# Key-value sums with v stationary in both 64-column halves of the PE array, turned back by ten PE transposes

## The chip, the cores and the metric

One core of a Trainium2 chip. The metric is the device time of one execution in microseconds (us), taken as the median of several. The profile of an execution has a span that is about 1.7 us shorter than its time.

Engines are called PE (TensorE matmul), PEld (its weight load), DVE (VectorE), ACT (ScalarE), POOL (GpSimd) and SP (SyncE, which issues the DMAs). PSUM is the memory to which PE writes its results; the kernel uses it as eight banks.

## The reference, cut to what matters

S is 2048 tokens, D is 640, 32 heads of 20 columns each. Only the key-value sums are changed:

```python
xn = layernorm(x)
q, k, v = split(xn @ wqkv)                       # 32 heads of 20
pk = einsum("hsd,hdf->hsf", k, w_phi)
phi_k = concat([softmax(pk), softmax(-pk)])      # per head 2 x 20 features: e+ and e-
kv = einsum("hsf,hsd->hfd", phi_k, v)            # the key-value sums
z  = einsum("hsf->hf", phi_k)
o  = (phi_q @ kv) / (phi_q @ z + 1e-6)
out = x + o @ wo + (silu(xn @ w1) * (xn @ w3)) @ w2
```

## The kernel before

All operations go through a small list scheduler in the kernel. Several streams (norms, attention, MLP tiles, output tiles and so on) each offer their next step; the scheduler estimates when each could start and commits the earliest. So an MLP tile (ten weight loads and ten matmuls, about 2.16 us of PE) is what fills PE whenever the attention stream is not ready. It also means that a change of one stage can move MLP tiles elsewhere.

The tokens are on the partitions. `ekt` holds the normalized e+ and e- of all tokens, `v2` holds v with a column of ones after each head's 20 columns (21 per head), so that the sum with the ones gives z. The kernel before makes e stationary and moves v, a full block of 128 features against the 7 or 8 heads that touch it, and masks out (`GM`) the products of features with foreign heads on the way to `KVc`, which the query tiles read:

```python
def kv_sum(sg, fc, k):                      # sg: e+ or e-; fc: one of five 128-feature chunks
    h0, h1 = heads_of_chunk(fc)
    nh = h1 - h0 + 1
    for t in range(T):                      # 16 tiles of 128 tokens
        mm(bank(k, 21 * nh), ekt[:, t, sg, fc * 128:(fc + 1) * 128],
           v2[:, t, 21 * h0:21 * (h1 + 1)], t == 0, t == T - 1)
    pv = bank(k, 21 * nh).rearrange("p (h c) -> p h c", c=21)
    g = GM[:, fc, h0:h1 + 1]
    kv = KVc[:, sg, fc, 0:22 * nh].rearrange("p (h c) -> p h c", c=22)
    tt("DVE", kv[:, :, 0:DH], pv[:, :, 0:DH], g.unsqueeze(2).to_broadcast([128, nh, DH]), ALU.mult)
    stt(kv[:, :, DH], pv[:, :, DH], DEN_EPS if sg == 0 else 0.0, g, ALU.add, ALU.mult)
    copy("POOL", kv[:, :, DH + 1], g)
```

The late constants and the attention stream around the sums:

```python
def consts_late():
    memset("POOL", v2[:].rearrange("p t (h c) -> p t h c", c=21)[:, :, :, DH], 1.0)
# ... attention():
    while done["n"] < T:                    # all keys normalized (POOL)
        yield None
    for fc in range(DC):
        for sg in range(2):
            yield lambda fc=fc, sg=sg: kv_sum(sg, fc, banks(1))
    done["kv"] = 1
    # ... loads of w2 and of two x tiles, then per token tile: q_tok (12 matmuls against KVc), q_proj
```

A warm-up keeps PE busy while the first tiles of x arrive. In this kernel it happens to contain, beside full 128x512 matmuls, pairs with 63 columns stationary in either half of the array and 120 columns moving: the very form that the change brings into use.

```python
for _ in range(8):
    for q in range(2):
        mm(PS[64 * q:64 * q + 63, 3584:3584 + 120], z[:, 0:63], z[:, 120 * q:120 * q + 120], True, True)
```

The softmax here doesn't subtract the row's maximum and nothing guards it: scores larger than these inputs give would overflow.

## Time and profile before

The time before was 281.79 us (median of 3, 281.46 to 282.14).

| stage of the profiled run | us from the start | what PE does |
|---|---|---|
| x loads, LN, first projections | 0 to 40 | waits for x in places |
| k and v projections, query projection | 40 to 73 | no gaps |
| four MLP tiles | 73 to 82 | fill, while the attention stream waits for POOL, which normalizes the keys |
| key-value sums | 82.15 to 92.82 | 160 matmuls |
| query tiles, projections, MLP tiles | 93 to 213 | no gaps |
| output tiles alone | 213 to 281 | no gaps |

The page of the kernel before: the span, the busy time of each engine, and the chain of waits (what ended last, followed back), by engine.

```profile
span 280.8 us, 4674 instructions
...
PE 274.1 (98%) x1905; PEld 169.5 (60%) x1923; DVE 182.5 (65%) x321; ACT 105.5 (38%) x190; POOL 59.2 (21%) x90
...
PE 95%; DMA 2%; SPq 1%; DVE 1%; issue 1%; ACT 0%
```

PE is busy 98% of the span and makes up 95% of the chain. A busy PE need not be a limit, because records of pipelined matmuls overlap (that of a 512-column matmul is 379 ns long, and the next starts after 216); that the chain runs through PE with breaks of only 0.05 us from 40.5 us on is the stronger sign.

The timeline of PE in the kernel before (start us, length us, what, count; neighbours of one kind are merged under the first one's shape):

```profile
6.28 1.06 PE L101 MATMUL PS<-t 128*63 128x120 bf16 x19
...
77.84 4.48 PE L101 MATMUL PS<-xnT,w_s 128*128 128x512 bf16 x19
82.15 10.83 PE L101 MATMUL PS<-v,ekt 128*128 128x147 bf16 x160
93.03 2.11 PE L101 MATMUL PS<-xnT,w_s 128*128 128x512 bf16 x9
94.98 0.85 PE L101 MATMUL PS<-KVc,EqT 128*128 128x154 bf16 x12
```

The whole stage is the second of the lower four lines. `PS<-xnT,w_s` are MLP tiles, `PS<-KVc,EqT` is the first query tile. One MLP tile between the sums and the first query tile is enough to wait for KVc. `x9` is a tile of ten of which the trace lacks one record, and it is the first one: from the start of the last sum to the first MLP record there are 281 ns, one sum of 64 and one 512-column matmul of 216 more. A later run has the kernel before with a change elsewhere (`e4_before_late_selects`); its trace has all ten records and confirms it, 82.78 to 93.44 us:

```profile
82.78 10.83 PE L101 MATMUL PS<-v,ekt 128*128 128x147 bf16 x160
93.44 2.32 PE L101 MATMUL PS<-xnT,w_s 128*128 128x512 bf16 x10
```

The other engines around the same stage, and POOL earlier on:

```profile
51.43 2.37 POOL L101 MEMSET v<- 128x512 bf16 x1
...
53.90 0.71 ACT L101 ACTIVATE v<-PS 128x640 bf16<-128x640 f32 x1 [0.48 <-POOL v L101]
...
54.40 27.05 POOL L101 TENSOR_TENSOR ekt<-ekt,rS 128x640 bf16<-128x640 bf16 x22 [0.60 <-DVE rS L101]
...
93.02 0.30 DVE L101 TENSOR_TENSOR KVc<-PS,GM 128x140 bf16<-128x140 f32 x1 [0.51 <-PE PS L101]
...
93.61 0.22 POOL L101 COPY KVc<-GM 128x7 bf16<-128x7 bf16 x1 [0.82 <-DVE KVc L101]
```

The square brackets give the idle time before an instruction and what ended it. KVc is complete at 93.83 us, 0.8 us after the last matmul. POOL's normalization of the keys (54.40 + 27.05) ends at 81.45 us, just before the sums can begin. The memset of the ones in `v2` sits in the middle of it, and ACT's copy of v waited 0.48 us for that.

### The profile page before, as it was taken

How to read it: one execution, taken by the hardware profiler on the slowest of the kernel's cores; microseconds unless marked ns; L12 is line 12 of the kernel's file. 1: busy time of each engine (PE TensorE's matmuls, PEld its weight loads, DVE VectorE, ACT ScalarE, POOL GpSimd, SP SyncE). 2: the span in 40 equal slices, each digit the busy share in tenths (PEclk: the TensorE clock that was granted, in tenths of full speed). 3: DMA queues.
4: the chain of work that ended last, by engine and by line, in shares of the span. 5: the costliest groups of instructions: out<-in, count | busy, mean ns of one | idle time of the engine just before them, and what ended most of it. 6: DMA issues, size and time to landing. Idle time of an engine off the chain costs nothing.

```text
span 280.8 us, 4674 instructions
## 1 busy us (share of the span) xinstructions
PE 274.1 (98%) x1905; PEld 169.5 (60%) x1923; DVE 182.5 (65%) x321; ACT 105.5 (38%) x190; POOL 59.2 (21%) x90
## 2 busy tenths in 40 slices
PE   8899989999999999999999999999999999999996
PEld 3656665776469655555555565744446777777774
DVE  5459879999664689989989997886663212121212
ACT  3377968787720354464464522132221000000000
POOL 4405397999961000000000000000000000000000
PEclk9999999999999999999999999999999999999999
DMA  7972899840000642111112124230000131222211
GB/s 200 292 215 46 140 326 254 104 120 0 0 2 0 207 145 44 30 23 26 23 33 40 23 47 50 57 83 4 0 0 2 48 92 60 83 68 75 71 49 47
DMA packets 40326, 21.96 MB, mean 78 GB/s; under 512 B 26736, under 2 KB 40304, under 8 KB 40304
## 3 DMA queue, kind: packets, MB, share of 16 engines
q1 hardware_dynamic: 40304, 21.66, 32.0%
q8 instruction: 15, 0.25, 0.4%
q14 instruction: 7, 0.06, 0.1%
HBM read 12.81 MB, written 2.62 MB: 55 GB/s over the span
## 4 chain that ended last, share of the span: by engine, by line
PE 95%; DMA 2%; SPq 1%; DVE 1%; issue 1%; ACT 0%
PE PS L101 95%; DMA x_tok<-in_A_x_dram 2%; SPq L113 1%; DVE bst L101 0%; ACT v L101 0%; DVE xres L101 0%; DVE x_tok L101 0%; DVE mv L101 0%
## 5 line engine op out<-in xcount | busy, mean ns | idle before, releaser
L101 PE MATMUL PS<-xnT,w_s 128*128 128x512 bf16 x467 | 105.2, 379 | 0.7
L101 PEld LDWEIGHTS PS<-xnT,w_s 128*128 128x128 bf16 x480 | 46.8, 98 | 55.4 <-ACT Wkp L101 0.2
L101 PE MATMUL PS<-w_s,hT 128*128 128x320 bf16 (+2 forms) x384 | 54.9, 299 | 0.0
L101 ACT ACTIVATE th<-PS 128x512 f32<-128x512 f32 x48 | 28.7, 599 | 56.3 <-PE PS L101 56.3
L101 DVE TENSOR_TENSOR xres<-PS,xres 128x640 bf16<-128x640 f32 (+2 forms) x17 | 13.4, 786 | 54.0 <-PE PS L101 54.0
L101 DVE SCALAR_TENSOR_TENSOR t<-th,PS 128x512 bf16<-128x512 f32 x48 | 32.9, 685 | 21.7 <-ACT th L101 21.7
L101 PEld LDWEIGHTS PS<-w_s,hT 128*128 128x128 bf16 x384 | 37.6, 98 | 14.6
L101 POOL TENSOR_TENSOR ekt<-ekt,rS 128x640 bf16<-128x640 bf16 x32 | 39.4, 1272 | 4.4 <-DVE rS L101 4.4
L101 DVE SCALAR_TENSOR_TENSOR hT<-t,PS 128x512 bf16<-128x512 bf16 x48 | 33.0, 687 | 1.6
L101 ACT ACTIVATE EqT<-PS 128x512 bf16<-128x512 f32 x40 | 21.7, 594 | 9.9 <-PE PS L101 9.9
L101 PE MATMUL PS<-Wkp,xnT 128*128 128x320 bf16 x160 | 23.9, 299 | 0.8 <-ACT v L101 0.8
L101 PE MATMUL PS<-wo_s,oT 128*128 128x320 bf16 (+2 forms) x160 | 24.5, 299 | 0.0
L101 DVE TENSOR_TENSOR prod<-PS,g_s 128x1280 bf16<-128x1280 f32 x16 | 23.9, 1491 | 0.5
L101 PE MATMUL PS<-wv,xnT 128*128 128x320 bf16 x160 | 24.2, 299 | 0.0
L101 ACT ACTIVATE ekt<-PS 128x640 bf16<-128x640 f32 x32 | 20.7, 713 | 7.0 <-PE PS L101 6.9
L101 DVE TENSOR_REDUCE S<-ekt 128x64 f32<-128x1280 bf16 x16 | 23.0, 1438 | 0.0
L101 PE MATMUL PS<-xnT,Wqp 128*128 128x512 bf16 x95 | 22.6, 379 | 0.3
L101 PEld LDWEIGHTS PS<-Wkp,xnT 128*128 128x128 bf16 x160 | 15.4, 98 | 7.1 <-ACT v L101 1.2
L101 PEld LDWEIGHTS PS<-wo_s,oT 128*128 128x128 bf16 x160 | 15.6, 98 | 6.1
L101 PEld LDWEIGHTS PS<-wv,xnT 128*128 128x128 bf16 x160 | 15.5, 98 | 5.8
L101 DVE BATCH_NORM_STATS2 bst<-x_tok 128x6 f32<-128x320 bf16 x32 | 15.3, 478 | 5.5 <-DMA x_tok<-in_A_x_dram 4.9
L101 ACT ACTIVATE e_s<-PS 128x64 f32<-128x64 f32 x32 | 9.0, 283 | 21.9 <-PE PS L101 20.9
(46 smaller groups left out, 169.0 us busy)
## 6 DMA issues: line engine op xcount, KB each, us to landing
w_s<-in_B_w_dram SPq DMA_DIRECT2D x6, 640.0 KB, 6.3
xres<-in_A_x_dram SPq DMA_DIRECT2D x16, 160.0 KB, 2.5
out_dram<-xres SPq DMA_DIRECT2D x15, 160.0 KB, 1.8
x_tok<-in_A_x_dram SPq DMA_DIRECT2D x3, 640.0 KB, 6.2
w_s<-in_B_w_dram SPq DMA_DIRECT2D x1, 1920.0 KB, 7.9
wv<-in_A_wqkv_dram SPq DMA_DIRECT2D x2, 400.0 KB, 4.8
wo_s<-in_A_wo_dram SPq DMA_DIRECT2D x1, 800.0 KB, 5.5
x_tok<-in_A_x_dram SPq DMA_DIRECT2D x4, 160.0 KB, 3.1
```

Source lines behind the costliest of these rows:

```text
L101: o = _Op(eng, lambda: m(*args, **kw), r, w, cost)
L113: o = _Op(eng, lambda: m(out, in_), self.regions(in_), self.regions(out), nbytes, True)
```

## The change

The intent is to use the array better. The two operands trade places: v with its ones, three heads (63 columns), becomes stationary, and e+ and e- of the same three heads (2 x 60 columns) move. Two such groups lie side by side, one in each 64-column half of the array, so that two matmuls can run at once. 11 groups of 16 token tiles make 176 matmuls. The result comes out transposed, so it is copied to a cleared staging tile (adding eps to the z rows on the way) and turned back by ten PE transposes; 15 masked products then write KVc. The warm-up is replaced by plain full matmuls. Not shown in the cut: KVc gets room for nine heads a chunk instead of eight, and the query tiles address it accordingly.

```diff
+    eps = new("eps", [128, 8], f32)
+    stg = new("stg", [128, 2, D], bf, RW + 3968)
     def consts_late():
+        memset("POOL", eps[:, 0:1], 0.0)
+        for p in (20, 41, 62, 84, 105, 126):
+            select(eps[:, 0:1], -p, [[0, 1]], 1, ALU.not_equal, DEN_EPS / 2)
         memset("POOL", v2[...][:, :, :, DH], 1.0)
-    def kv_sum(sg, fc, k):                       # cut: see above
+    def kv_sum(pairs, k):
+        for n, p in enumerate(pairs):
+            groups = [g for g in (2 * p, 2 * p + 1) if 3 * g < H]
+            for t in range(T):
+                for g in groups:
+                    q, nh = g % 2, min(3, H - 3 * g)
+                    o = PS[64 * q:64 * q + 21 * nh, k * 512 + 120 * n:k * 512 + 120 * n + 40 * nh]
+                    ...
+                    mm(o.rearrange("p (s f) -> p s f", s=2), v2[:, t, 63 * g:63 * g + 21 * nh],
+                       ekt[:, t, :, 60 * g:60 * g + 20 * nh], t == 0, t == T - 1, True, ...)
+        ...                                      # copies to stg on ACT or DVE, eps added
+    def kv_store(chunks, k):
+        for n, fc in enumerate(chunks):
+            for sg in range(2):
+                c = k * 1024 + 256 * n + 128 * sg
+                tr(PSb[:, c:c + 128], stg[:, sg, 128 * fc:128 * fc + 128])
+        for n, fc in enumerate(chunks):
+            ...
+            for g in range(g0, min(g0 + 3, 11)):
+                ...
+                tt("DVE", o[:, :, :, 0:DH + 1], i,
+                   m.unsqueeze(1).unsqueeze(3).to_broadcast([128, 2, nh, DH + 1]), ALU.mult)
+            ...                                  # one POOL copy of the mask per chunk
     # attention():
-        for fc in range(DC):
-            for sg in range(2):
-                yield lambda fc=fc, sg=sg: kv_sum(sg, fc, banks(1))
+        yield lambda: memset("POOL", stg[:], 0.0)
+        yield lambda: kv_sum((0, 1, 2, 3), banks(1))
+        yield lambda: kv_sum((4, 5), banks(1))
+        yield lambda: kv_store((0, 1, 2), banks(1))
+        yield lambda: kv_store((3, 4), banks(1))
     # warm-up: 10 and 4 matmuls of 128x512 instead of the mixture before
```

More of the change, by code (lines that the diff above doesn't have):

```diff
@@ L324, in bass_parallel_sum__linear_kernel_hedgehog__glu_gated_swiglu__prompt_kernel @@
     e_s = new("e_s", [128, 2, 4, H], f32, RV + 20480)
-    RW = region(12800)
+    RW = region(12928)
     wqkT = new("wqkT", [128, 2 * DC, D], bf, RW)
-    KVc = new("KVc", [128, 2, DC, 8 * 22], bf, RW)
-    prod = new("prod", [128, 2, 2, D], bf, RW + 3520)
-    o_tok = new("o_tok", [128, 3, D], bf, RW + 8640)
+    KVc = new("KVc", [128, 2, DC, 9 * 22], bf, RW)
+    stg = new("stg", [128, 2, D], bf, RW + 3968)
+    prod = new("prod", [128, 2, 2, D], bf, RW + 3968)
+    o_tok = new("o_tok", [128, 3, D], bf, RW + 9088)
     EqT = [EqT0, EqT1]
@@ L341, in bank2, with mm @@
         return PS[:, k * 512:(k + 2) * 512].rearrange("p (b c) -> p b c", c=512)[:, :, 0:cols]
-    def mm(o, l, r, start, stop, shared=False):
-        n = r.shape[-1]
+    def mm(o, l, r, start, stop, shared=False, cost=None):
+        n = free(r)
         P.op("PE", "matmul", [o], [l, r], (o, l, r),
-             dict(start=start, stop=stop, skip_group_check=shared), cost=max(n / 2400 + 0.003, 0.055))
+             dict(start=start, stop=stop, skip_group_check=shared),
+             cost=max(n / 2400 + 0.003, 0.055) if cost is None else cost)
     def tr(o, i, idn=None):
@@ L456, in ln_apply, with warm_up @@
                  cost=0.9)
-    def warm_up(first):
+    def warm_up(n, first):
         z = t1[:, 2, :]
@@ L462, in warm_up @@
             memset("DVE", z, 0.0)
-            for _ in range(8):
-                mm(bank(7), z[:, 0:128], z, True, True)
-            for _ in range(8):
-                for q in range(2):
-                    mm(PS[64 * q:64 * q + 60, 3584:3584 + 63], z[:, 0:60], z[:, 0:63], True, True)
-            for _ in range(4):
-                mm(bank(7, 128), z[:, 0:128], z[:, 0:128], True, True)
-        else:
-            for _ in range(8):
-                for q in range(2):
-                    mm(PS[64 * q:64 * q + 63, 3584:3584 + 120], z[:, 0:63], z[:, 120 * q:120 * q + 120],
-                       True, True)
-            for _ in range(3):
-                mm(bank(7, 240, 0, 126), z[:, 0:126], z[:, 0:240], True, True)
+        for _ in range(n):
+            mm(bank(7), z[:, 0:128], z, True, True)
     def xn_transpose(t, k):
@@ L535, in k_norm @@
                ALU.mult)
-    def kv_sum(sg, fc, k):
-        h0, h1 = heads_of_chunk(fc)
-        nh = h1 - h0 + 1
-        for t in range(T):
-            mm(bank(k, 21 * nh), ekt[:, t, sg, fc * 128:(fc + 1) * 128],
-               v2[:, t, 21 * h0:21 * (h1 + 1)], t == 0, t == T - 1)
-        pv = bank(k, 21 * nh).rearrange("p (h c) -> p h c", c=21)
-        g = GM[:, fc, h0:h1 + 1]
-        kv = KVc[:, sg, fc, 0:22 * nh].rearrange("p (h c) -> p h c", c=22)
-        tt("DVE", kv[:, :, 0:DH], pv[:, :, 0:DH], g.unsqueeze(2).to_broadcast([128, nh, DH]), ALU.mult)
-        stt(kv[:, :, DH], pv[:, :, DH], DEN_EPS if sg == 0 else 0.0, g, ALU.add, ALU.mult)
-        copy("POOL", kv[:, :, DH + 1], g)
+    def kv_sum(pairs, k):
[5 more added lines that the diff above has]
+                    o = PS[64 * q:64 * q + 21 * nh, k * 512 + 120 * n:k * 512 + 120 * n + 40 * nh]
+                    first, last = n == 0 and t == 0, p == pairs[-1] and t == T - 1
+                    mm(o.rearrange("p (s f) -> p s f", s=2), v2[:, t, 63 * g:63 * g + 21 * nh],
+                       ekt[:, t, :, 60 * g:60 * g + 20 * nh], t == 0, t == T - 1, True,
+                       (0.09 if first or last else 0.0) + (0.0265 if len(groups) == 2 else 0.053))
+        full = [p for p in pairs if 6 * p + 6 <= H]
+        for q in range(2):
+            i = PS[64 * q:64 * q + 63, k * 512:k * 512 + 120 * len(full)]
+            o = stg[64 * q:64 * q + 63, :, 120 * full[0]:120 * full[0] + 120 * len(full)]
+            kv_copy(o.rearrange("p s (n q f) -> p n s q f", q=2, f=60)[:, :, :, q, :],
+                    i.rearrange("p (n s f) -> p n s f", s=2, f=60), eps[64 * q:64 * q + 63, 0:1])
+        if len(full) < len(pairs):
+            c = k * 512 + 120 * len(full)
+            kv_copy(stg[0:42, :, 600:640], PS[0:42, c:c + 80].rearrange("p (s f) -> p s f", s=2),
+                    eps[0:42, 0:1])
@@ new lines, in kv_copy @@
+    def kv_copy(o, i, e):
+        n = free(o)
+        a = P.free["ACT"] + 0.17 + n / 1200
+        d = P.free["DVE"] + 0.14 + n / 960
+        if a <= d:
+            P.op("ACT", "activation", [o], [i, e], (o, i, ACT.Identity), dict(bias=e), cost=0.17 + n / 1200)
+        else:
+            P.op("DVE", "tensor_scalar", [o], [i, e], (), dict(out=o, in0=i, scalar1=e, scalar2=None,
+                 op0=ALU.add), cost=0.14 + n / 960)
+    def kv_store(chunks, k):
[4 more added lines that the diff above has]
+        for n, fc in enumerate(chunks):
+            g0 = heads_of_chunk(fc)[0] // 3
+            ps = PSb[:, k * 1024 + 256 * n:k * 1024 + 256 * n + 256].rearrange("p (s c) -> p s c", s=2)
+            for g in range(g0, min(g0 + 3, 11)):
+                nh = min(3, H - 3 * g)
+                i = ps[:, :, 64 * (g % 2):64 * (g % 2) + 21 * nh].rearrange("p s (h c) -> p s h c", c=21)
+                o = KVc[:, :, fc, 66 * (g - g0):66 * (g - g0) + 22 * nh]
+                o = o.rearrange("p s (h c) -> p s h c", c=22)
+                m = GM[:, fc, 3 * g:3 * g + nh]
+                tt("DVE", o[:, :, :, 0:DH + 1], i,
+                   m.unsqueeze(1).unsqueeze(3).to_broadcast([128, 2, nh, DH + 1]), ALU.mult)
+            nh = min(9, H - 3 * g0)
+            o = KVc[:, :, fc, 0:22 * nh].rearrange("p s (h c) -> p s h c", c=22)[:, :, :, DH + 1]
+            copy("POOL", o, GM[:, fc, 3 * g0:3 * g0 + nh].unsqueeze(1).to_broadcast([128, 2, nh]))
@@ L565, in q_tok @@
                 h0, h1 = heads_of_chunk(fc)
+                g0 = h0 // 3 * 3
                 for q in range(2):
@@ L570, in q_tok @@
                            EqT[b % 2][:, sg, fc, 128 * j:128 * j + 128],
-                           KVc[:, sg, fc, 22 * (lo - h0):22 * (hi - h0)],
+                           KVc[:, sg, fc, 22 * (lo - g0):22 * (hi - g0)],
                            first[q], fc == DC - 1 or (q == 0 and fc == 2), True)
@@ L708, in v @@
             return lambda: v_tile(t, banks(2))
-        yield lambda: warm_up(True)
+        yield lambda: warm_up(10, True)
         yield from transposed(0)
-        yield lambda: warm_up(False)
+        yield lambda: warm_up(4, False)
         yield from transposed(1)
```

## The prediction

> **What bounds the kernel now.** TensorE. The page shows PE busy 98% of 280.8 us; the chain of waits puts 95% of the span on PE matmuls, and from 40.5 us to the last output tile its only breaks are issue gaps of 0.05 us. The clock is full. In the windows from 93.03 to 203 us VectorE (DVE) is busy 86%. So PE time removed counts nearly one to one while gated MLP tiles are left to fill PE's waits; in the timeline only 9 of 48 precede the key-value sums, and 10 follow the last query tile.
>
> **Removed.** The timeline has the key-value sums as one gapless run of 160 matmuls, 82.15 to 93.03 us (10.88 us), 64 ns from start to start at 147 columns.
>
> **Added, in PE time.**
> - 80 pairs, each 63 columns of v stationary in either half of the array, 120 columns moving. The old warm-up contains this form: pairs start every 52.5 ns, halves 2 to 3 ns apart, weight loads hidden. [...] 2 to 3 ns between halves, and 150 to 200 ns between starts at the change of form against 56 without. 80 x 52.5 = 4.2 us.
> - The last group, two heads alone: 16 matmuls of 80 columns. The 88-column query matmuls start 38 ns apart; I estimate 36 to 53 ns: 0.6 to 0.85 us.
> - 10 transposes at 56 ns (as the x transposes): 0.56 us.
> - Switches: about 0.4 us (estimate from the 150 to 200 ns).
>
> Sum 6.0 us for 10.88: PE saves about 4.9 us.
>
> **Off PE.** DVE before: ten products of 304 ns, ten sums of 191 ns, 5.0 us. After: 15 products of about 0.3 us (estimate from those) and part of the copies to staging; about the same, but later. From the last pair to a complete KVc I expect 4 to 6 us against 0.8; two or three MLP tiles of 2.15 us, pulled forward, should cover it. POOL: six one-column selects, a memset and the clearing of staging, 2 to 3 us (estimate from selects of 0.3 us and a memset of 0.2 us on 128 columns). POOL is 100% busy from 60 to 78 us and its key normalization ends at 81.45 us, just before the sums, so these may start 1 to 2 us later; one more MLP tile fills that. The memset of v also comes later, so ScalarE's v copy, which waited 0.5 us for it, may wait 2 us; at most a few tenths reach PE. The warm-up changes form only: 10 cold matmuls of 427 ns end before the first transpose at 5.90 us, and the chain there runs through the x load.
>
> **Time.** 281.8 - 4.9 + 0.1 of new gaps = 277.0 us, 1.7% faster; range 276.0 to 278.2. 2% would need 5.6 us, more than the block can give, unless the new order also closes gaps elsewhere.
>
> **What would show it.** Timeline: pair spacing 52 to 53 ns; sums and transposes about 6 us of PE; MLP tiles between second sum, transposes and first query tile; PE idle unchanged (about 6.7 us in all); the tail of output tiles still 75 us.
>
> **What would make it wrong.** Halves that run in turn when accumulating or moving two strips of 60 columns (+4 us); weight loads that show; a PE gap over 0.5 us before the first query tile or at the v copy; the program's list scheduler ordering later stages otherwise, half a us either way.

The sum is 4.2 + 0.6 to 0.85 + 0.56 + 0.4, about 6.0 us, and the 0.4 us rests on the 150 to 200 ns of the trace alone.

## The result, and the profile after

| | median us | range us | runs |
|---|---|---|---|
| before | 281.97 | 281.46 to 282.35 | 4 |
| after | 277.70 | 277.36 to 279.12 | 4 |

The ratio is 0.9859 (95% interval 0.9821 to 0.9898). Ratios here are the mean time of one kernel's runs over the mean of the other's in the same rounds, so not quite the ratio of the medians. The predicted 277.0 us is 0.7 us too low, and the measured time lies in the range of 276.0 to 278.2. Two later batches with more rounds put the ratio at 0.9845 (277.81 us against 282.41) and 0.9825 (278.02 against 282.51), so the change is worth about 4.5 us, 1.6%.

The page of the changed kernel:

```profile
span 275.8 us, 4687 instructions
...
PE 269.7 (98%) x1916; PEld 163.3 (59%) x1916; DVE 182.1 (66%) x319; ACT 106.3 (39%) x192; POOL 60.3 (22%) x93
...
PE 81%; DVE 7%; DMA 5%; POOL 3%; SPq 2%; issue 1%; ACT 1%; POOLq 0%; ACTq 0%
```

PE is as busy as before, in a span shorter by 5.0 us. The chain's share on PE fell from 95% to 81%, and that is not because PE has become less of a limit: the chain is followed back from the end, and where it meets one short wait of PE it leaves PE and follows the engine that was waited for all the way back. The wait that it met is told below.

PE's timeline of the changed kernel around the sums:

```profile
73.43 10.95 PE L101 MATMUL PS<-xnT,w_s 128*128 128x512 bf16 x50
84.32 4.96 PE L101 MATMUL PS<-ekt,v 128*63 128x120 bf16 x176
89.31 0.51 PE L101 MATMUL PS<-ident,stg 128*128 128x128 bf16 x6
89.65 2.32 PE L101 MATMUL PS<-xnT,w_s 128*128 128x512 bf16 x10
91.81 0.39 PE L101 MATMUL PS<-ident,stg 128*128 128x128 bf16 x4
92.03 13.11 PE L101 MATMUL PS<-xnT,w_s 128*128 128x512 bf16 x60
104.98 0.86 PE L101 MATMUL PS<-KVc,EqT 128*128 128x154 bf16 x12
```

From start to next start, the sums take 84.32 to 89.31 = 4.99 us and the transposes 0.34 and 0.22 us: 5.55 us where 10.66 stood, 5.1 us less. One MLP tile more than before precedes the sums (five instead of four from 73 us on), and seven follow before the first query tile instead of one. PE has no gap through all of it.

An account of the 5.0 us between the two spans, by PE's starts: up to the start of the sums nothing (82.15 us before, 84.32 after, less one MLP tile of 2.16); sums and transposes -5.1 us; from there to the end +0.1 us. That last term has its cause in the records: the 88-column query matmuls start 40.4 instead of 38.3 ns apart on average, 64 times, 0.14 us.

The zero of the first term is a sum of things that cancel. The third tile of x was ready 0.4 us earlier and the wait for loads at 39 us was 0.4 us shorter in this run. Against that stand the wait that the chain met (0.7 us) and 0.09 us at the change of form before the first pair. That the loads came early is luck of this one profile. What does not depend on them is the time from the first sum to the end: 191.49 to 191.50 us in six traces with the changed order (this one, both controls, the old warm-up and both early-selects runs), 198.64 and 198.65 us with the old order, where one MLP tile more (2.16 us) follows the sums. That leaves 5.0 us. The chain of waits of the changed kernel in order of time (start us, length us, what), leaving out short pieces:

```profile
50.84 0.19 POOL eps L101
...
52.77 2.31 POOL v L101
...
55.17 0.71 ACT v L101
...
56.53 32.75 PE PS L101 x343
89.31 184.00 PE PS L101 x1201
```

POOL and PE there, from the changed kernel's timeline:

```profile
51.28 1.50 POOL L101 TENSOR_SCALAR_AFFINE_SELECT eps<-eps 128x1 f32<-128x1 f32 x5 [0.25 <-POOL eps L101]
52.71 2.37 POOL L101 MEMSET v<- 128x512 bf16 x1
...
55.94 0.49 PE L101 MATMUL PS<-BDc,wqkT 128*128 128x140 bf16 x6 [0.28 <-ACT v L101]
```

The six selects come before the memset of the ones, the memset ends at 55.08 us instead of 53.80, ACT's v copy waited 2.57 us for it instead of 0.48, and PE waited for that copy to free its PSUM banks. Computed from the starts of single matmuls, PE stood 0.44 us before this group and 0.27 us behind it: 0.71 us, where the kernel before had nothing.

The way from the sums to KVc on ACT, DVE and POOL:

```profile
87.91 1.34 ACT L101 ACTIVATE stg<-PS,eps 63x480 bf16<-63x480 f32 x2 [3.97 <-PE PS L101]
89.32 1.05 DVE L101 TENSOR_SCALAR stg<-PS,eps 63x120 bf16<-63x120 f32 x3 [3.93 <-PE PS L101]
90.29 0.92 DVE L101 TENSOR_TENSOR KVc<-PS,GM 128x126 bf16<-128x126 bf16 x3
...
97.32 0.25 POOL L101 COPY KVc<-GM 128x16 bf16<-128x16 bf16 x1 [1.00 <-DVE KVc L101]
```

KVc is complete at 97.57 us, 8.3 us after the last matmul of the sums. Before it was 0.8 us.

### The profile page after: what moved, and what is told of

It is laid out like the page before. It is cut to its first block, busy times and chain, and to the rows that moved or that the text cites. A ratio compares the mean times of both kernels' runs of the same rounds, so it can differ in the third digit from the quotient of the medians. Undisturbed runs are those within 1.5% of the kernel's fastest.

```text
span 275.8 us, 4687 instructions
## 1 busy us (share of the span) xinstructions
PE 269.7 (98%) x1916; PEld 163.3 (59%) x1916; DVE 182.1 (66%) x319; ACT 106.3 (39%) x192; POOL 60.3 (22%) x93
## 4 chain that ended last, share of the span: by engine, by line
PE 81%; DVE 7%; DMA 5%; POOL 3%; SPq 2%; issue 1%; ACT 1%; POOLq 0%; ACTq 0%
PE PS L101 81%; DMA x_tok<-in_A_x_dram 5%; DVE bst L101 4%; POOL ekt L101 2%; SPq L113 2%; DVE mv L101 1%; POOL v L101 1%; DVE S L101 1%; DVE hT L101 0%; DVE t L101 0%; POOL eps L101 0%; ACT v L101 0%; DVE x_tok L101 0%; ACT th L101 0%; ACT Wqp L101 0%
## 5 line engine op out<-in xcount | busy, mean ns | idle before, releaser
L101 PE MATMUL PS<-xnT,w_s 128*128 128x512 bf16 x480 | 107.0, 379 | 0.0
L101 PE MATMUL PS<-xnT,Wqp 128*128 128x512 bf16 x100 | 23.7, 379 | 0.0
```

What stands on the lines that cost most here:

```text
L101: o = _Op(eng, lambda: m(*args, **kw), r, w, cost)
```

## The experiments

Twelve runs of ten kernels were made in three batches of four. Kernels are compared only within the same rounds. Within a batch all share the runs of the kernel before, and the changed kernel itself (or, in the second batch, the early-selects kernel) was run again as a control.

| run | median us | ratio to before (95%) |
|---|---|---|
| a0_after, control | 277.81 | 0.9845 (0.9821 to 0.9869) |
| e1_halves_in_turn | 280.11 | 0.9917 (0.9896 to 0.9938) |
| e3_eps_early | 277.12 | 0.9809 (0.9786 to 0.9831) |
| e4_before_late_selects | 283.71 | 1.0048 (1.0022 to 1.0075) |
| e8_one_half | 282.13 | 0.9982 (0.9951 to 1.0014) |
| e9_blocks_of_four | 278.00 | 0.9836 (0.9800 to 0.9872) |
| e7_both | 276.52 | 0.9782 (0.9755 to 0.9810) |
| e3b_eps_early, control | 277.03 | 0.9808 (0.9781 to 0.9835) |
| a1_after, control | 278.02 | 0.9825 (0.9792 to 0.9858) |
| e2_old_warmup | 277.75 | 0.9817 (0.9784 to 0.9849) |
| e5_products_twice | 280.31 | 0.9908 (0.9875 to 0.9942) |
| e10_no_fill | 285.35 | 1.0090 (1.0051 to 1.0130) |

The kernel before had 282.41, 282.45 and 282.51 us in the three batches.

### The control

> The changed kernel again, as the control of this batch: ratio to the kernel before 0.983 (0.981 to 0.986); the run of paired key-value matmuls about 5.0 us, transposes 0.56 us. If the run-to-run spread of the first result (277.4 to 279.1 us) comes from the loads of x, single times move with the arrival of the x tiles and not with the key-value stage.

Ratio 0.9845, the run of pairs again 4.99 us. The loads do move: in this run the wait before the third x tile was 1.10 us and that at 39 us 0.33 us, against 0.86 and 0.60 in the first profile. So differences of a few tenths between single profiles in the first 40 us are not the change's.

### Where the 5.1 us come from: halves in turn

```diff
-            for t in range(T):
-                for g in groups:
+            for g in groups:
+                for t in range(T):
```

> The same instructions, but all 16 matmuls of one half of the array before those of the other half, so that no two halves can run together. Theory (most of the gain is that the halves run at the same time): 160 matmuls at 52.5 ns or a little more = 8.4 us and 0.6 us for the last group, so the run lasts 9.0 us instead of 5.0 and the time is 4.0 us longer than the changed kernel's (ratio to before about 0.997). Rival (the gain is from the swap: 120 columns moving instead of 147 and narrow weight loads, and alternation does not matter): the run stays 5 us, ratio 0.983.

The run of pairs in this kernel's timeline:

```profile
85.07 7.37 PE L101 MATMUL PS<-ekt,v 128*63 128x120 bf16 x176
```

It took 7.3 us to the next start, neither 9.0 nor 5.0, and the time rose by 2.3 us, just what the run grew. So PE time in this stage counts one to one, but both theories missed the size. The starts of single matmuls show why. At each change of half (ns from one start to the next, from the trace's records):

```
... 52  53  52  53  52   6  47  31  21  32  21  31  53  52  53 ...
```

While one half works alone the starts are 52.5 ns apart. Then two series run beside each other, each at 52.5 ns: the first matmuls of the next half start before the last three of the old half have started. Sixteen matmuls thus took 662 ns instead of 16 x 52.5 = 840. The rows of the trace do not name the half, so this is read from the spacing. It needed two more runs.

### One half only, and blocks of four

The first writes every group into the lower half, so that nothing can run beside anything; its result is wrong (relative error 0.39). The second changes halves after every four matmuls, because three or four overlapped at each change above.

```diff
-                    q, nh = g % 2, min(3, H - 3 * g)
+                    q, nh = 0, min(3, H - 3 * g)
```

> A wrong result on purpose: all groups write the lower half of the array (order of instructions as in the changed kernel), so nothing can run beside anything. Theory (halves run side by side, and the run with the halves one after the other took only 7.4 us because PE starts three or four matmuls of the next half before the last ones of the other have started): 160 x 52.5 ns + 0.6 us = 9.0 us for the run, time 4.0 us over the changed kernel, ratio to before about 0.997. Rival (a queue or load limit, not the halves, set the 7.4 us): 7.4 us again.

```diff
-            for t in range(T):
-                for g in groups:
+            for t4 in range(0, T, 4):
+                for g, t in [(g, t) for g in groups for t in range(t4, t4 + 4)]:
```

> Blocks of four matmuls of one half, then four of the other. Theory [...]: nearly all pairs still overlap, run 5.0 to 5.3 us, ratio as the changed kernel. Rival (only neighbours pair up; the overlap in the halves-in-turn run is something that happens once per change of 16): about one in four overlaps, run 7 us or more.

The runs of pairs, first with one half, then with blocks of four:

```profile
84.83 9.16 PE L101 MATMUL PS<-ekt,v 128*63 128x120 bf16 x176
```

```profile
85.02 4.96 PE L101 MATMUL PS<-ekt,v 128*63 128x120 bf16 x176
```

With one half the stage took 9.1 us and the time was 282.13 us, 4.1 us above the blocks-of-four kernel of the same rounds, which is as fast as the changed kernel: as the theory said. The ratio to before, 0.9982, is not clear of 1. (With one half, two groups also sum into the same place in PSUM. That this is not what slows them is seen in the kernel before: its sums go 16 times in a row into one place, at 64 ns for 147 columns, nearly the same time per column as 52.5 ns for 120.) With blocks of four the stage took 5.07 us (85.02 to the transposes at 90.09) and the time was 278.00. From the first to the last start it was 4.76 us, exactly as in the changed kernel: in blocks of four all of them paired up. In program order, with 52.5 ns between starts in one half, four and four would have taken at least 6 x 52.5 = 315 ns; the starts show 210 ns for eight. By what means PE departs from that order is not shown. So the gain splits: trading places alone, without pairing, would have taken the stage from 10.66 to 9.1 us, which the transposes and the new waits use up; running two halves at once gives the remaining 4.1 us.

### The selects on POOL

The first moves the memset and the six selects of `eps` to the time before the block diagonal is built, where POOL waits for a load. The second puts them, unused, into the kernel before.

```diff
-        yield block_diag
+        yield consts_eps          # the memset and the six selects, no longer in consts_late
+        yield block_diag
```

> The memset and the six one-column selects moved from the late constants (ahead of the memset of v, in the middle of the key normalization) to an idle stretch of POOL before the block diagonal is built. Theory (the 2.1 us of selects delay the memset of v, ScalarE's v copy waits for it, and PE loses 0.44 + 0.27 us near 55 us): those two gaps go, POOL ends its normalization 2 us earlier, and the time falls by 0.5 to 0.8 us against the changed kernel (ratio to before about 0.981). Rival (the gaps come from the order of instructions or from the Wqp fold): the gaps stay, no change beyond 0.2 us.

```diff
 # kernel before
     def consts_late():
+        memset("POOL", eps[:, 0:1], 0.0)
+        for p in (20, 41, 62, 84, 105, 126):
+            select(eps[:, 0:1], -p, [[0, 1]], 1, ALU.not_equal, DEN_EPS / 2)
```

> The kernel before with the six selects and the memset of eps added to its late constants, result unused. Theory: it gets the same two PE gaps near 55 us and is 0.5 to 0.8 us slower than before (ratio 1.002 to 1.003). Rival: no change (ratio 1.000) and no gap over 0.2 us there.

With early selects, POOL and PE near 55 us look like this:

```profile
51.00 2.36 POOL L101 MEMSET v<- 128x512 bf16 x1
...
54.55 1.52 PE L101 MATMUL PS<-wv,xnT 128*128 128x320 bf16 x10
55.91 0.48 PE L101 MATMUL PS<-BDc,wqkT 128*128 128x140 bf16 x6
```

Each group follows the one before it without a bracket: both gaps are gone. The time fell by 0.7 us against the control of its rounds (277.12 against 277.81), inside the expected 0.5 to 0.8. The kernel before with late selects got the same two gaps (0.45 and 0.27 us) and was 1.3 us slower by the medians; one of its six executions had the clock at 0.994 (285.1 us). The interval of the ratio (1.0022 to 1.0075) reaches down into the expected 1.002 to 1.003, so a size beyond the 0.7 us of gaps is not shown. Both ways round, the selects cost PE time, though POOL is off the critical path by its share of busy time.

### The warm-up

The warm-up of the kernel before was put back into the changed kernel (the `warm_up` function and its two calls as before).

> The changed kernel with the warm-up matmuls of the kernel before. Theory (the first stage waits for the x loads): no change beyond 0.3 us against the control. Rival (the new warm-up brings the first stage forward by the 0.4 us by which the third x transpose came earlier in the first profiles): 0.3 to 0.5 us slower than the control.

277.75 us against the control's 278.02: within the expected 0.3 us. The rival, that the new warm-up is part of the gain, falls.

### The way from the sums to KVc: work doubled, filling forbidden

```diff
-                tt("DVE", o[:, :, :, 0:DH + 1], i, ...)
+                for _ in range(2):
+                    tt("DVE", o[:, :, :, 0:DH + 1], i, ...)
```

> Every masked product of key-value sums into KVc is made twice (the second writes the same again): 4.7 us more of VectorE work between the transposes and the first query tile. Theory (that latency is covered by MLP tiles pulled forward): KVc complete some 5 us later, one MLP tile more before the first query tile, time within 0.5 us of the control. Rival (the latency from the sums to KVc is on the critical path): 2 to 5 us slower.

```diff
 # mlps(): a tile must also wait
+   or done["hold"] and not done["q"]      # hold is set just before the first kv_sum is offered
```

> No MLP tile may be ordered between the start of the sums and the first query tile (one that is already at hand slips in between the two groups of transposes; six are moved to after the last query tile). Theory (the change lengthens the way from the last sum to a complete KVc to about 7 us, and only the filling hides it): PE idles 4 to 5.5 us before the first query tile, time 4 to 5 us over the control, ratio to before about 1.000, so the whole gain is gone. Rival (VectorE is idle enough that KVc is ready soon): under 1 us slower.

PE of the kernel with doubled products:

```profile
92.91 4.48 PE L101 MATMUL PS<-xnT,w_s 128*128 128x512 bf16 x20
98.29 3.41 PE L101 MATMUL PS<-xnT,w_s 128*128 128x512 bf16 x15 [0.90 <-DVE t L101]
103.04 7.73 PE L101 MATMUL PS<-xnT,w_s 128*128 128x512 bf16 x35 [1.34 <-DVE KVc L101]
```

This expectation was wrong. The time rose by 2.3 us over the control (280.31 against 278.02), and the two gaps, 0.90 and 1.34 us, add up to it. They do not stand in front of a query tile, where the rival would have them, but in the run of MLP tiles. The filling itself needs DVE. The first gap ends with a DVE pass of an MLP tile (`t`): each tile has two such passes of 0.69 us before its PSUM banks are free, and behind 1.9 us of products they come too late. The second gap ends with the last product itself (`KVc`). Fifteen matmuls, a tile and a half, stand before it; by the kernel's schedule, the half tile that follows writes the PSUM bank that holds the last four transposes, and that bank is free only when their products are done. So the wait is hidden only as long as DVE can serve both. The changed kernel has little to spare there: DVE works almost without a gap from 90.3 to 104 us.

PE of the kernel in which no MLP tile may fill:

```profile
92.28 0.23 PE L101 MATMUL PS<-KVc,EqT 128*128 128x154 bf16 x1
93.16 0.24 PE L101 MATMUL PS<-KVc,EqT 128*128 128x154 bf16 x1 [0.65 <-POOL KVc L101]
94.46 0.26 PE L101 MATMUL PS<-KVc,EqT 128*128 128x88 bf16 x2 [1.06 <-POOL KVc L101]
96.63 0.31 PE L101 MATMUL PS<-KVc,EqT 128*128 128x154 bf16 x1 [1.92 <-POOL KVc L101]
97.88 0.97 PE L101 MATMUL PS<-KVc,EqT 128*128 128x154 bf16 x7 [0.94 <-POOL KVc L101]
98.64 3.88 PE L101 MATMUL PS<-xnT,Wqp 128*128 128x512 bf16 x10
```

And two windows of it (length; busy time and count of PE, PEld, DVE, ACT, POOL; then the granted clock, the DMA share and GB/s):

```profile
92.00:98.00 6.00, 1.44 (x13) 0.71 (x11) 4.47 (x14) 0.00 (x0) 1.04 (x4) 0.75 0.98 339
98.00:102.00 4.00, 4.00 (x16) 1.94 (x16) 2.63 (x6) 1.55 (x4) 0.00 (x0) 0.53 0.01 4
```

Here the time was 285.35 us, 7.3 us over the control and 0.9% slower than before the change. The expected idle time is there: the starts of single matmuls leave 0.81 + 1.23 + 2.09 + 1.18 = 5.3 us of gaps. The other 2 us were not expected, and they are the clock. Its record falls to 0.5 at 94.95 us and is back at 1.0 at 101.78. Seven starts of the first query projections are 427 ns apart instead of 216, which is 1.5 us; the query matmuls before them and the change back to the full clock add 0.4 us. The clock fell 2.6 us after PE's last gapless work, with three query matmuls in between; what made it fall just then is not shown. So without MLP tiles to pull forward this change would have been a loss.

### A version that is faster than both

The early selects are kept, and the ten PE transposes are replaced by two DMA transposes of the staging tile. Because the scheduler would otherwise put 34 MLP tiles before the first query tile (in a build that was not run), the attention stream's DVE steps were also given priority; the kernel that ran has twelve.

```diff
-                tr(PSb[:, c:c + 128], stg[:, sg, 128 * fc:128 * fc + 128])
+        for sg in range(2):
+            yield lambda sg=sg: P.dma("SP", KVT[:, sg], stg[:, sg, :], True)
-    URGENT = {0: 4.0, 3: 4.0}
+    URGENT = {0: 4.0, 2: 8.0, 3: 4.0}
```

> The early selects, and the ten PE transposes replaced by two DMA transposes of staging, with the attention stream's VectorE steps made urgent for the list scheduler. Theory (PE time is the time): PE loses 10 transposes and their change of form, 0.7 us, and the latency of the DMA (2 to 3 us) is covered by MLP tiles: 0.6 us under the early-selects kernel of the same rounds, ratio about 0.979. Rival (the transposes hide in gaps that PE has anyway): no difference.

> The early-selects kernel again, as the control of this batch: ratio 0.981 (0.979 to 0.983) to the kernel before.

PE goes straight from the pairs to MLP tiles, while two DMAs turn the sums:

```profile
83.88 4.96 PE L101 MATMUL PS<-ekt,v 128*63 128x120 bf16 x176
88.78 1.47 PE L101 MATMUL PS<-xnT,w_s 128*128 128x512 bf16 x6
...
89.96 2.53 SPq L113 DMA_TRANSPOSE KVT<-stg  x2
```

The median is 276.52 us (275.90 to 276.62) against the control's 277.03 (276.96 to 277.45): 0.5 us less, ranges apart, close to the expected 0.6. The ratio to before is 0.9782 (0.9755 to 0.9810), 2.2% faster, though the interval does not clear 2%. This is the fastest correct kernel, and the transposes were on PE's path. The run changes two things against that control, the transposes and the priority of DVE steps. The traces leave little for the second: from the first pair to the end 190.81 us pass against 191.50, 0.69 us less, and the transposes (0.56 us) with the 0.10 us of the longer gap before them account for 0.66 us.

The last control, for completeness:

> The changed kernel as the control of this batch: ratio to before 0.984 (0.982 to 0.987).

It came to 0.9825.

## Why the prediction was right

- **What bounds.** Right. Each stretch added to or taken from PE came back in the time: the run of pairs 2.3 us longer gave 2.3 us (halves in turn), 4.1 us longer gave 4.1 (one half).
- **Removed and added PE time.** Right in the mechanism; two sizes were off in the same direction, and that they cancel in the difference is luck. Predicted 10.88 us out and 6.0 in, saving 4.9. Measured 10.66 out (the prediction counted the missing MLP record as part of the sums) and 5.64 in (5.55, and 0.09 on entering the new form), saving 5.0. The pairs started 52.5 ns apart, as the warm-up had shown, and the halves 2 to 3 ns apart. A weight load of 63 columns took 109 ns in the records, one of 128 columns 98; that cost nothing here. The last group ran at 35 to 36 ns, the low end of the estimate. The changes of form were over-sized: 0.4 us was set down. Entering took 0.09 us (310 ns from the start of a 512-column matmul to the first pair instead of 216) and leaving 0.10 (134 ns from the start of an 80-column matmul to the next instead of 36, in three runs where nothing else was waited for). The gap before the transposes of the changed kernel is 0.20 us because they also wait for ACT's copy to staging, which ends at 89.25 us.
- **Halves at the same time.** Right, and shown: 5.0 us with both halves, 9.1 us with one.
- **Way to KVc.** Under-sized. "4 to 6 us" was 8.3, and not "two or three" but seven MLP tiles came before the first query tile. The products took what was estimated (0.29 us in the mean), but they queue behind the MLP tiles' own DVE passes, and DVE waits 0.36 us for POOL's copy between chunks in places. It cost nothing here because filling was at hand. The runs with doubled products and without filling show that this was the weakest step: doubling exposed 2.2 us, and without filling all was lost and more.
- **POOL.** The mechanism was right, its size low. The prediction let "at most a few tenths" of the later memset reach PE; it was 0.7 us, and moving the selects got 0.7 us back. The sums did start one MLP tile later, as said.
- **Time.** 277.0 predicted. The terms measured make 281.8 - 5.0 + 0.7 + 0.1 = 277.6; the median was 277.7 in the first batch. The 0.7 us by which the prediction was low is nearly all the gap behind POOL, 0.7 instead of 0.1. So close an agreement is partly chance: single profiles differ by some tenths through the loads alone.
- **Warm-up and tail.** Right: old warm-up within 0.3 us. From the start of the last MLP matmul to the end 67.6 us pass in both profiles; the 75 us of the prediction would begin at 205.8 us, where the last MLP tiles still run. PE's idle time, forecast as unchanged at 6.7 us, was 6.1 (275.8 - 269.7).

## What to carry to other kernels

Before a new matmul form is built, look whether some part of the kernel already runs it: eight warm-up pairs gave the rate of the new stage to a nanosecond. A stage that becomes shorter on the bounding engine but gets a longer tail on others is paid for with filling; count who else the filling needs, since here MLP tiles left PE gaps of 0.90 and 1.34 us once DVE, with the products doubled, freed their banks too late. Small constants on an engine that is "off the path" belong where that engine waits: six selects of 0.19 us, placed ahead of a memset that others wait for, cost 0.7 us of the bounding engine.
